# Splitting a block of the next matrix product behind the sum of two PSUM banks, with other places for attention in a tiled attention and two-layer kernel

## The chip, the cores and the metric

One core of a Trainium2 chip runs the whole kernel. The metric is the device time of one launch in microseconds. TensorE (PE in the profile) does the matrix products, VectorE (DVE) and ScalarE (ACT) the elementwise work, GpSimd (POOL) one power per pair of rows and a part of the DMA issues, SyncE (SP) the other DMA issues. The kernel before takes 1167.32 us, the median of three runs (1164.36 to 1168.64).

## What is computed

```
out  = softmax(q k / 8) v          # 4 x 8 heads, 768 rows, chunks of 32 with 16 left, 8 right, 8 memory keys
x    = out as 3072 x 512
xn   = x / sqrt(mean(x * x) + 1e-6) * rms_g
y    = (silu(xn @ w_gate) * (xn @ w_val)) @ w_out          # 512 -> 1536 -> 512
h    = y @ w_in                                            # 512 -> 2048
g    = where(h >= 1, h, where(h <= -1, 0, (h + 1)**2 / 4))
out  = g @ w_out                                           # 2048 -> 512
```

## The kernel before

The 3072 rows are six tiles of 512. Every fp32 operand of a product is held as two parts, a high one and what is left of it (`xh` and `xl`, `wh` and `wl`, `r[:, 0]` and `r[:, 1]`), and three matmuls (high by high, high by low, low by high) stand for one product of 128 x 128 by 128 x 512.

**Attention** is done in twelve pairs of 256 rows. A pair has nine steps: `s0`, `s1` (scores), `a0`, `a1` (transposes of the exponentials), `v0`, `v1` (weighted sums), `r0` (row scales, on ACT for all pairs but the first two, L526), `x0`, `x1` (transposes of the normalized rows, L540, copied out on ACT at L553). All of them write one PSUM tile, `ps_a`, of two banks.

**The first layer of tiles 0 to 3** runs in the loop at L832, twelve values of `f` each: the gate product `proj_in(ps_g[0])`, the value product `proj_in(ps_g[1])`, and the output product `out1` of the `f` before. Each is twelve matmuls. After each of the three stands a slot, `slot(t, s)` with s from 0 to 35; it runs at most one step of attention (`att_slot`, from the tables `plan`, `plan2` and `plan3`) and some steps of weight preparation (`conv_step`, or `conv_w` in tile 0). The tables give the slot of each step: in tile 0 by hand, later one pair per eleven slots (`plan2`). In tile 0 the order on PE and SP is the program's, and a scheduler orders DVE, ACT and POOL; from tile 1 on all engines take the order of the program. At the end of a tile `split_x` (L354) makes the two parts of the next tile's rows. `load_y` (L775) loads the rows of the last two tiles for what follows, and `x_steps` (L803) turns them into the sums below, one step per slot from `f` 8 of the last tile on.

**The first layer of the last two tiles and the whole second layer** use a scheme with seven half-size products in place of eight, for two tiles at once (called a pair of tiles here). `seven(n, early)` at L890 does one block of columns: products 0 to 6 of six matmuls each, on five PSUM banks. In the order of its code: products 0 (bank A) and 1 (C); ACT copies A to B (L898) and C to `p5` (L899); then everything in the list `defer`; product 2 adds to B, product 3 adds to A; DVE writes C = p5 + B (L906, the sum of banks of the title); `early` starts the activation of A; everything in `defer2`; product 4 adds to B; DVE adds B to `p5` (L912); product 5 adds to C; product 6 adds to B. So product 4 has to wait until L906 has read B, and product 6 until L912 has. `proj1` calls it for the first layer (12 blocks), `proj2` for the second (3 times 8 blocks); `conv_step` puts weight preparation between the products in `proj1`.

The output product of a pair of tiles is `Out.run` at L1001. It goes through blocks n, each with a split of one block of `h` into a ring buffer: `Out.split` (L984) is an ACT copy (L991), a DVE subtraction (L993) and, for the first blocks, a DVE sum (L995). The first few splits are done ahead, while `seven` still runs: `ahead` (L1051) puts them in `defer`, so that the next call of `seven` takes them. Four blocks are split so in `proj1`, and four in each of the three rounds of `proj2`, 16 in all.

Of the kernel before, what the change touches and what calls it, by code (L numbers as in the profile page):

```python
# [8 lines left out]
F32 = mybir.dt.float32  # L9
# [7 lines left out]
P = 128  # L17
# [13 lines left out]
TT = 512  # L31
# [3 lines left out]
PACE = (2.2, 2.9, 2.9, 3.1, 2.2, 2.9, 3.1, 4.2, 2.9, 4.2, 3.2)  # L35
# [4 lines left out]
def tile_stream_attention_moe_moe2(  # L40
# [14 lines left out]
    KK = DM // P  # L55
# [7 lines left out]
    att_only = ctx.enter_context(ExitStack())  # L63
# [41 lines left out]
    ps_a = apool.tile([P, 2, 512], F32, name="ps_a")  # L105
    ps_g = [psum.tile([P, 512], F32, name=f"ps_g{i}") for i in range(2)]
    y_d = [dram.tile([P, KK, TT], F32, name=f"y_d{t}") for t in range(NTT)]
    x_d = {t: dram.tile([P, KK, TT], F32, name=f"x_d{t}") for t in range(2, NTT)}
    NS = NTT - 2
# [52 lines left out]
    def conv_w():  # L162

        n = len(absd)
        if f32s:
            conv_hi()()
        if raw:
            conv_c()
        if n:
            conv_d()  # L170
# [168 lines left out]
    m2 = {"single": True, "pace": 0.0, "hold": False}  # L339
# [176 lines left out]
    def part_p(pr):  # L516
        rs = small.tile([P, 2], F32, tag="rs", name="rs")
        nc.gpsimd.tensor_tensor(out=rs, in0=ss_t.pop(2 * pr + 1), in1=nhalf, op=ALU.pow)
        rs_t[pr] = rs
# [11 lines left out]
            )  # L531

    def step_x(pr, blk, ps):

        t, o = divmod(pr, 2)
        if t == 1 and t not in xn_t:
            xn_t[t] = xs.tile([P, KK, TT], F32, tag="xn", name="xn")
        x = x_t[pr]
        for kk in range(KK):
            nc.tensor.transpose(ps[:, kk * P:(kk + 1) * P], x[blk][:, kk * P:(kk + 1) * P], ident)  # L540
        ps_t["x", pr, blk] = ps

    def part_X(pr, blk):
        t, o = divmod(pr, 2)
        ps = ps_t.pop(("x", pr, blk))
        c0 = (2 * o + blk) * P
        if t < 2:
            xn = xn_t[t][:, :, c0:c0 + P]
        else:
            xn = x_t[pr][blk].rearrange("p (k i) -> p k i", k=KK)  # L550
        rows = ps.rearrange("p (k i) -> p k i", k=KK)
        for kk in range(KK):
            nc.scalar.activation(xn[:, kk], rows[:, kk], AF.Copy, scale=g_t[:, kk:kk + 1])  # L553
        if t >= 2:
            nc.sync.dma_start(x_d[t][:, :, c0:c0 + P], xn)
# [69 lines left out]
    for st in ORDER.split():  # L625
        c, n = st[0], st[1:]
# [3 lines left out]
        n = int(n)  # L630
# [51 lines left out]
    mpsum = ctx.enter_context(tc.tile_pool(name="mpsum", bufs=1, space=bass.MemoryType.PSUM))  # L682
    ps_y.extend(mpsum.tile([P, 512], F32, name=f"ps_y{i}") for i in range(4))

    plan = {1: "s0", 3: "a0", 4: "v0", 7: "s1", 9: "a1", 10: "v1", 11: "r0", 14: "x0", 15: "x1"}

    plan2 = {0: "s0", 3: "a0", 4: "s1", 5: "v0", 6: "a1", 8: "v1", 11: "r0", 12: "x0", 13: "x1"}
    plan3 = {0: "s0", 3: "a0", 4: "s1", 5: "v0", 6: "a1", 7: "v1", 9: "r0", 10: "x0", 11: "x1"}  # L690

    def att_slot(t, s):
        if t == 0:
            o, r = divmod(s, 18)
            if r in plan:
                att_step(2 + o, plan[r])
            return

        if s == 34:
            return  # L700
        s += 36 * (t - 1)
        s -= (s > 34) + (s > 70)
        for pr in range(4, 2 * NTT):

            st = (plan3 if pr == 2 * NTT - 1 else plan2).get(s - 11 * (pr - 4))
            if st is not None:
                att_step(pr, st)

    def att_step(pr, st):
        n = int(st[1])  # L710
        if st[0] in "sav" and f"{st[0]}{2 * pr + n}" in done:
            return
        if st[0] == "x":
            step_x(pr, n, ps_a[:, n])
            part_X(pr, n)
        elif st[0] == "r":
            step_r(pr)
        else:
            u = 2 * pr + n
            fns[st[0]](u, ps_a)  # L720
            for p in parts[st[0]]:
                fn = (lambda p=p: fns[p](u)) if p != "p" else (lambda: part_p(pr) if n else None)
                if pr < 4 or p in "mAn":
                    fn()
                else:
                    (later if p in "kp" else after).append(fn)
        if st[0] == "s":
            load_qk(2 * pr + n + 1)
        if st[0] == "v":
            load_v(2 * pr + n + 1)  # L730
# [3 lines left out]
    def conv_step(n):  # L734
        m2["pace"] += n
        while m2["pace"] >= 1:
            m2["pace"] -= 1
            if m2["hold"] and not live:
                continue
            for fn in bg.pop() if bg else ():  # L740
                fn()

    def slot(t, s):
        late = later[:]
        later.clear()
        att_slot(t, s)
        for fn in late:
            fn()
        if t == 0:
            conv_w()  # L750
            load_w(units1, 1)
        else:
            if xq:
                xq.pop(0)()
            m2["hold"] = t == NS - 1 and s >= 29
            n = s + 36 * (t - 1)
            conv_step(1 if s > 32 else PACE[(n - (n > 34) - (n > 70)) % 11] if n < 92 else 2.5)
            for fn in after:
                fn()
            after.clear()  # L760
# [14 lines left out]
    def load_y(*src):  # L775
        for o in range(2):
            nc.sync.dma_start(m2["y"][:, o], src[o])
# [54 lines left out]
    for t in range(NS):  # L832
        if t == 1:
            region.close()
            region.enter_context(tc.manual_schedule())
        for f in range(F1):
            if t == NS - 1 and f == F1 - 1:
                for i in range(8):
                    load_wp(i)
            proj_in(ps_g[0], w1[("g", f)])  # L840
            s = sp.tile([P, TT], F32, tag="s", name="s")
            nc.scalar.activation(s, ps_g[0], AF.Silu)
            if t == NS - 1 and f == 8:
                xq.extend(x_steps())
            slot(t, 3 * f)
            if 0 < t < NS - 1 and f == 9:
                load_x(t + 1)
            if t == NS - 1 and f == 6:
                att_only.close()
                right = ctx.enter_context(tc.tile_pool(name="right", bufs=1, side="right", reuse_waits="tile"))  # L850
                m2["y"] = right.tile([P, 2, KK, TT], F32, name="y")
                load_y(x_d[NS], x_d[NS + 1])
            proj_in(ps_g[1], w1[("v", f)])
            if f == F1 - 1 and t + 1 < NS:
                split_x(xn_t.pop(t + 1))
            nc.vector.tensor_tensor(out=s, in0=s, in1=ps_g[1], op=ALU.mult)
            low = split_h(f, s)
            if t == 0:
                low()
            slot(t, 3 * f + 1)  # L860
            if t:
                low()
            if pend is not None:
                out1(*pend)
            pend = (t, f)
            slot(t, 3 * f + 2)
# [21 lines left out]
    banks, defer, defer2 = [], [], []  # L888
# [162 lines left out]
    def ahead(o, n, last):  # L1051
        if last:
            o.ahead(n)
        else:
            defer.append(lambda: o.ahead(n))

    def done1(j, o, bank, p5):

# [205 lines left out]
```

## Time and profile before

| | |
|---|---|
| median of three runs | 1167.32 us |
| the profiled execution, its own time | 1166.26 us |
| its span, first to last instruction | 1164.5 us |
| granted TensorE clock, mean | 0.987 of full speed |
| PE, DVE, ACT, POOL busy | 97%, 70%, 53%, 9% |

The span is cut into stages by the trace: up to 34 us the first attention alone, tile 0 up to 150, tiles 1 to 3 up to 497, `proj1` up to 614, its output product up to 700, and then three rounds of `proj2` with its output product. A matmul of 512 columns lasts 0.39 us in the profile, and the next starts 0.23 us after it started; since the ends overlap, idle time of PE is told shorter in the profile than what it costs. The columns of each view are named where its rows stand.

### The profile page before, as it was taken

How to read it: one execution, taken by the hardware profiler on the slowest of the kernel's cores; microseconds unless marked ns; L12 is line 12 of the kernel's file. 1: busy time of each engine (PE TensorE's matmuls, PEld its weight loads, DVE VectorE, ACT ScalarE, POOL GpSimd, SP SyncE). 2: the span in 40 equal slices, each digit the busy share in tenths (PEclk: the TensorE clock that was granted, in tenths of full speed). 3: DMA queues.
4: the chain of work that ended last, by engine and by line, in shares of the span. 5: the costliest groups of instructions: out<-in, count | busy, mean ns of one | idle time of the engine just before them, and what ended most of it. 6: DMA issues, size and time to landing. Idle time of an engine off the chain costs nothing.

```text
span 1164.5 us, 20927 instructions
## 1 busy us (share of the span) xinstructions
PE 1125.2 (97%) x7879; PEld 908.8 (78%) x7879; DVE 819.1 (70%) x1433; ACT 617.5 (53%) x1088; POOL 102.9 (9%) x152
## 2 busy tenths in 40 slices
PE   6999999999999999999989999999999999999998
PEld 4677787877787778887778887788887788877886
DVE  4887577767656765756656867797677887577855
ACT  3886656646665774444334534456344465344553
POOL 0200003221221222111110000000000000000000
PEclk6999999999999999999999999999999999999999
DMA  8976358998968877799987797666777667762564
GB/s 295 325 236 207 101 182 276 306 330 302 297 217 313 285 249 245 253 322 380 391 314 221 215 320 249 193 181 196 236 206 254 173 198 216 216 194 81 157 190 160
DMA packets 144212, 281.81 MB, mean 242 GB/s; under 512 B 15216, under 2 KB 65392, under 8 KB 142320
## 3 DMA queue, kind: packets, MB, share of 16 engines
q1 hardware_dynamic: 123664, 228.57, 61.6%
q0 software_dynamic: 12768, 43.52, 10.8%
q10 hardware_dynamic: 7680, 8.39, 2.1%
q8 instruction: 62, 1.02, 0.4%
q14 instruction: 38, 0.31, 0.1%
HBM read 201.26 MB, written 79.17 MB: 241 GB/s over the span
## 4 chain that ended last, share of the span: by engine, by line
PE 81%; DVE 6%; ACT 5%; DMA 5%; issue 2%; SPq 0%; POOL 0%; ACTq 0%; DVEq 0%; POOLq 0%
PE ps_y L1043 14%; PE ps_g L1043 11%; PE ps_g L564 6%; PE ps_g L566 6%; PE ps_g L565 6%; PE ps_b L879 4%; PE ps_g L879 4%; PE ps_b L881 3%; PE ps_b L880 3%; PE ps_g L881 3%; PE ps_g L880 3%; PE ps_y L564 3%; PE ps_y L565 3%; PE ps_y L566 3%; DMA w<-in_w_dram 2%
## 5 line engine op out<-in xcount | busy, mean ns | idle before, releaser
L1043 PE MATMUL ps_y<-r,wo 128*128 128x512 f32 x672 | 156.2, 390 | 0.0
L564 PE MATMUL ps_g<-xh,wall 128*128 128x512 f32 x384 | 155.5, 405 | 0.7 <-ACT wall L158 0.3
L993 DVE TENSOR_TENSOR r<-h,r 128x512 fp32r<-128x512 f32 x167 | 112.2, 688 | 61.8 <-ACT r L991 61.8
L566 PE MATMUL ps_g<-xh,wall 128*128 128x512 f32 x384 | 150.2, 391 | 0.7 <-DVE wall L160 0.7
L565 PE MATMUL ps_g<-xl,wall 128*128 128x512 f32 x384 | 150.2, 391 | 0.6 <-DVE xl L659 0.4
L1043 PEld LDWEIGHTS ps_y<-r,wo 128*128 128x128 f32 x672 | 125.6, 188 | 26.0
L944 ACT ACTIVATE t<-t,half 128x512 f32<-128x512 f32 x96 | 66.9, 720 | 126.6 <-DVE t L943 120.9
L991 ACT ACTIVATE r<-h 128x512 fp32r<-128x512 f32 x167 | 100.7, 625 | 56.2 <-DVE r L993 17.5
L1043 PE MATMUL ps_g<-r,wo 128*128 128x512 f32 x498 | 116.0, 390 | 0.0
L1043 PEld LDWEIGHTS ps_g<-r,wo 128*128 128x128 f32 x498 | 93.2, 188 | 19.4 <-DVE r L993 0.2
L566 PEld LDWEIGHTS ps_g<-xh,wall 128*128 128x128 f32 x384 | 72.1, 188 | 17.4 <-DVE wall L160 1.6
L564 PEld LDWEIGHTS ps_g<-xh,wall 128*128 128x128 f32 x384 | 72.1, 188 | 17.0 <-ACT wall L158 1.0
L879 PE MATMUL ps_g<-wall 128*128 128x512 f32 x198 | 78.5, 397 | 7.0 <-DVE ps_y L906 3.2
L565 PEld LDWEIGHTS ps_g<-xl,wall 128*128 128x128 f32 x384 | 72.2, 188 | 14.7 <-DVE xl L659 0.7
L879 PE MATMUL ps_b<-wall 128*128 128x512 f32 x202 | 79.8, 395 | 3.5 <-DVE ps_g L906 3.5
L881 PE MATMUL ps_b<-wall 128*128 128x512 f32 x202 | 79.1, 392 | 0.0
L880 PE MATMUL ps_b<-wall 128*128 128x512 f32 x202 | 79.1, 392 | 0.0
L564 PE MATMUL ps_y<-hh,wall 128*128 128x512 f32 x192 | 77.8, 405 | 0.0
L881 PE MATMUL ps_g<-wall 128*128 128x512 f32 x198 | 77.3, 390 | 0.0
L880 PE MATMUL ps_g<-wall 128*128 128x512 f32 x198 | 77.2, 390 | 0.0
L565 PE MATMUL ps_y<-hl,wall 128*128 128x512 f32 x192 | 75.1, 391 | 0.0
L566 PE MATMUL ps_y<-hh,wall 128*128 128x512 f32 x192 | 74.9, 390 | 0.0
(201 smaller groups left out, 2086.8 us busy)
## 6 DMA issues: line engine op xcount, KB each, us to landing
wo<-w2o_d SPq DMA_DIRECT2D x88, 512.0 KB, 3.6
wall<-w2p_d SPq DMA_DIRECT2D x168, 256.0 KB, 3.0
wall<-w1p_d SPq DMA_DIRECT2D x84, 256.0 KB, 6.2
w<-in_w_dram POOLq DMA_DIRECT2D x32, 512.0 KB, 5.7
w<-in_w_dram SPq DMA_DIRECT2D x30, 512.0 KB, 5.2
k_in<-in_k_dram SPq DMA_DIRECT2D x48, 256.0 KB, 5.1
wo<-w1o_d SPq DMA_DIRECT2D x21, 512.0 KB, 3.6
v_in<-in_v_dram SPq DMA_DIRECT2D x40, 260.0 KB, 4.2
```

The lines of the kernel that those rows point to most:

```text
L564: nc.tensor.matmul(ps, wh, xh, start=start, stop=False)
L565: nc.tensor.matmul(ps, wh, xl, start=False, stop=False)
L566: nc.tensor.matmul(ps, wl, xh, start=False, stop=stop)
L879: nc.tensor.matmul(bank, wh, xh, start=st, stop=False, skip_group_check=True)
L880: nc.tensor.matmul(bank, wh, xl, start=False, stop=False, skip_group_check=True)
L881: nc.tensor.matmul(bank, wl, xh, start=False, stop=kk == 1, skip_group_check=True)
L944: nc.scalar.activation(s, s, AF.Square, scale=0.5, bias=half)
L991: nc.scalar.activation(r[:, 0], src, AF.Copy)
L993: tt_(out=r[:, 1], in0=src, in1=r[:, 0].bitcast(F32), op=ALU.subtract)
L1043: nc.tensor.matmul(bank[p][m], a, b, start=s0, stop=s1, skip_group_check=True)
```

## The change

Five things, of which the first is a single word:

- `ahead` puts the split of a block into `defer2` in place of `defer`.
- The table `plan` of tile 0 names slots for both pairs by hand; the pairs' steps stand further apart (`a` to `v` two slots in place of one, `x0` to `x1` two in place of one) and begin two slots sooner.
- In `plan2`, the row scales `r0` stand at slot 10 of a pair in place of slot 11.
- Of the last three tiles, the second tile of the program keeps slots 33 and 34 free of attention (before, 34 alone), the third slot 34 as before. From there on attention runs one slot later, and so does `load_y`, which moves from behind slot 18 of the last tile to behind slot 19.
- `step_x` writes bank 0 of `ps_a` for `x1` too, where it wrote bank 1.

```diff
     def att_slot(t, s):
         if t == 0:
-            o, r = divmod(s, 18)
-            if r in plan:
-                att_step(2 + o, plan[r])
+            if s in plan:
+                att_step(*plan[s])
             return
 
-        if s == 34:
+        s += 36 * (t - 1)
+        if s in (33, 34, 70):
             return
-        s += 36 * (t - 1)
-        s -= (s > 34) + (s > 70)
+        s -= 2 * (s > 34) + (s > 70)
...
-    plan = {1: "s0", 3: "a0", 4: "v0", 7: "s1", 9: "a1", 10: "v1", 11: "r0", 14: "x0", 15: "x1"}
+    plan = {
+        1: (2, "a0"), 3: (2, "v0"), 4: (2, "s1"), 7: (2, "a1"), 9: (2, "v1"), 11: (2, "r0"), 12: (2, "x0"), 14: (2, "x1"),
...
-    plan2 = {0: "s0", 3: "a0", 4: "s1", 5: "v0", 6: "a1", 8: "v1", 11: "r0", 12: "x0", 13: "x1"}
+    plan2 = {0: "s0", 3: "a0", 4: "s1", 5: "v0", 6: "a1", 8: "v1", 10: "r0", 12: "x0", 13: "x1"}
...
-            step_x(pr, n, ps_a[:, n])
+            step_x(pr, n, ps_a[:, 0])
...
     def ahead(o, n, last):
         if last:
             o.ahead(n)
         else:
-            defer.append(lambda: o.ahead(n))
+            defer2.append(lambda: o.ahead(n))
```

In the rows below, lines of the changed kernel are one lower than those of the kernel before (L905 is the sum of banks L906, L992 the subtraction L993).

DVE in `proj2`, block 4 of the first round, before: `r0` is a ring buffer of the split, `ps_g0`, `ps_g1` and `ps_y3` are banks C, B and A of this call, `t0` is `p5`.

```order
L921 TENSOR_TENSOR h_7248<-h_7248 128x512
L993 TENSOR_TENSOR r0_7239<-h_7248,r0_7239 128x512
L995 TENSOR_TENSOR h_7248<-h_7248 128x512
L906 TENSOR_TENSOR ps_g0_111<-t0_7232,ps_g1_112 128x512
L943 TENSOR_SCALAR t1_7233<-ps_y3_706 128x512
L912 TENSOR_TENSOR t0_7232<-t0_7232,ps_g1_112 128x512
L948 TENSOR_TENSOR h_7248<-t1_7233,ps_y3_706 128x512
```

The same place in the changed kernel:

```order
L920 TENSOR_TENSOR h_7248<-h_7248 128x512
L905 TENSOR_TENSOR ps_g0_111<-t0_7232,ps_g1_112 128x512
L942 TENSOR_SCALAR t1_7233<-ps_y3_706 128x512
L992 TENSOR_TENSOR r0_7239<-h_7248,r0_7239 128x512
L994 TENSOR_TENSOR h_7248<-h_7248 128x512
L911 TENSOR_TENSOR t0_7232<-t0_7232,ps_g1_112 128x512
L947 TENSOR_TENSOR h_7248<-t1_7233,ps_y3_706 128x512
```

The two operations of the split moved from ahead of the sum of banks to a place between the activation of A and the second sum, L912 (now L911).

ACT at that place, before: L898 and L899 are the two copies of `seven`, L944 the square of the activation, L991 the copy of the split.

```order
L898 ACTIVATE ps_g1_112<-ps_y3_706 128x512
L899 ACTIVATE t0_7232<-ps_g0_111 128x512
L991 ACTIVATE r0_7239<-h_7248 128x512
L944 ACTIVATE t1_7233<-t1_7233,half_103 128x512
L944 ACTIVATE t2_7234<-t2_7234,half_103 128x512
```

And in the changed kernel:

```order
L897 ACTIVATE ps_g1_112<-ps_y3_706 128x512
L898 ACTIVATE t0_7232<-ps_g0_111 128x512
L943 ACTIVATE t1_7233<-t1_7233,half_103 128x512
L990 ACTIVATE r0_7239<-h_7248 128x512
L943 ACTIVATE t2_7234<-t2_7234,half_103 128x512
```

The split's copy now stands behind the square of A, whose input DVE makes from product 3.

ACT at the end of the second tile, before: L526 are the row scales of a pair, L438 the exponential of the next pair's scores with its table load, L356 the split of the next tile's rows, L553 the copies out of `x0`.

```order
L526 ACTIVATE x_nat_3012<-x_nat_3012,rs_3176 128x512
L526 ACTIVATE x_nat_3013<-x_nat_3013,rs_3176 128x512
L203 ACTIVATE wgv_3185<-s1234_3188 128x512
L438 ACT_TABLE_LOAD
L438 ACTIVATE e_3259<-e_3259 128x512
L356 ACTIVATE xh_582<-xn_3038 128x512 x4
L579 ACTIVATE hh_3290<-s_3221 128x512
L553 ACTIVATE x_nat_3012<-ps_a_110,g_t_108 128x128 x4
```

In the changed kernel:

```order
L526 ACTIVATE x_nat_3012<-x_nat_3012,rs_3176 128x512
L526 ACTIVATE x_nat_3013<-x_nat_3013,rs_3176 128x512
L203 ACTIVATE wgv_3185<-s1234_3188 128x512
L841 ACTIVATE s_3223<-ps_g0_111 128x512
L203 ACTIVATE wgv_3185<-s1234_3188 128x512
L356 ACTIVATE xh_582<-xn_3038 128x512 x4
L578 ACTIVATE hh_3247<-s_3223 128x512
L438 ACT_TABLE_LOAD
L438 ACTIVATE e_3300<-e_3300 128x512
L841 ACT_TABLE_LOAD
L841 ACTIVATE s_3324<-ps_g0_111 128x512
L552 ACTIVATE x_nat_3012<-ps_a_110,g_t_108 128x128 x4
```

The exponential moved from ahead of the split of the tile's rows to behind it, and the row scales went ahead of the gate's activation (L842, now L841).

## Rows read from the trace of the kernel before

**Rows 1.** The page: busy us of each engine, share of the span and instructions.

```profile
PE 1125.2 (97%) x7879; PEld 908.8 (78%) x7879; DVE 819.1 (70%) x1433; ACT 617.5 (53%) x1088; POOL 102.9 (9%) x152
```

**Rows 2.** Waits of PE, 34 to 150 us: us in total, times, longest.

```profile
PE ps_a L459 <- ACT aT L449: 2.3, 2, 1.2
PE ps_g L566 <- DVE wall L160: 0.7, 1, 0.7
PE ps_a L443 <- ACT e L438: 0.6, 1, 0.6
PE ps_a L540 <- ACT xn L553: 0.3, 1, 0.3
```

**Rows 3.** Waits of PE, 150 to 497 us.

```profile
PE ps_a L540 <- ACT x_nat L553: 2.5, 4, 1.3
PE ps_a L540 <- DVE e L429: 0.4, 1, 0.4
PE ps_g L564 <- ACT xh L356: 0.3, 1, 0.3
```

**Rows 4.** Waits of PE, 497 to 614 us.

```profile
PE ps_y L879 <- DVE ps_b L906: 2.0, 1, 2.0
PE ps_g L879 <- DVE ps_b L906: 2.0, 1, 2.0
PE ps_b L879 <- DVE ps_g L906: 1.7, 2, 1.3
PE ps_g L879 <- DVE ps_y L906: 1.3, 1, 1.3
```

**Rows 5.** Waits of PE, 614 to 1164 us, one of four such rows.

```profile
PE ps_y L879 <- DVE ps_b L906: 1.8, 3, 0.6
```

**Rows 6.** Timeline of PE, DVE, ACT from 714 us: start us, us, what, [idle before <-releaser].

```profile
714.12 0.39 PE L879 MATMUL ps_b<-wall 128*128 128x512 f32 x1
...
714.32 0.69 DVE L943 TENSOR_SCALAR t<-ps_g 128x512 f32<-128x512 f32 x1 [0.59 <-PE ps_g L881]
...
715.05 0.72 ACT L944 ACTIVATE t<-t,half 128x512 f32<-128x512 f32 x1 [2.79 <-DVE t L943]
...
715.68 0.69 DVE L912 TENSOR_TENSOR t<-t,ps_b 128x512 f32<-128x512 f32 x1 [0.67 <-PE ps_b L881]
```

**Rows 7.** Timeline of ACT and DVE around the split in the next block.

```profile
719.42 0.72 ACT L944 ACTIVATE t<-t,half 128x512 f32<-128x512 f32 x1 [0.74 <-DVE t L943]
720.05 0.58 ACT L898 ACTIVATE ps_g<-ps_y 128x512 f32<-128x512 f32 x1
721.18 0.60 ACT L899 ACTIVATE t<-ps_g 128x512 f32<-128x512 f32 x1 [0.55 <-PE ps_g L881]
721.67 0.62 ACT L991 ACTIVATE r<-h 128x512 fp32r<-128x512 f32 x1
...
722.33 0.69 DVE L993 TENSOR_TENSOR r<-h,r 128x512 fp32r<-128x512 f32 x1 [0.86 <-ACT r L991]
723.05 0.69 DVE L995 TENSOR_TENSOR h<-h 128x512 f32<-128x512 f32 x1
723.66 0.69 DVE L906 TENSOR_TENSOR ps_g<-t,ps_g 128x512 f32<-128x512 f32 x1
```

**Rows 8.** Timeline of PE at the same block's product 4.

```profile
723.41 0.39 PE L881 MATMUL ps_y<-wall 128*128 128x512 f32 x1
724.41 0.50 PE L879 MATMUL ps_g<-wall 128*128 128x512 f32 x1 [0.60 <-DVE ps_g L906]
```

**Rows 9.** Timeline of DVE in block 7 of `proj2`, first round.

```profile
756.14 1.22 DVE L819 TENSOR_TENSOR y<-y 128x1024 f32<-128x1024 f32 x1
757.37 0.69 DVE L912 TENSOR_TENSOR t<-t,ps_g 128x512 f32<-128x512 f32 x1
```

**Rows 10.** Windows: us, busy us (x) of PE, PEld, DVE, ACT, POOL, PEclk, DMA.

```profile
608.60:612.00 3.40, 3.40 (x10) 2.63 (x9) 1.29 (x2) 0.31 (x1) 1.05 (x2) 0.50 0.72 212
```

**Rows 11.** Timeline of DVE at the first step of `x_steps` in the last tile.

```profile
467.93 1.23 DVE L819 TENSOR_TENSOR y<-y 128x1024 f32<-128x1024 f32 x1 [4.07 <-DMA y<-x_d]
```

More of the change, by code (lines that the diff above doesn't have):

```diff
@@ L683, in tile_stream_attention_moe_moe2 @@
     ps_y.extend(mpsum.tile([P, 512], F32, name=f"ps_y{i}") for i in range(4))
-    plan = {1: "s0", 3: "a0", 4: "v0", 7: "s1", 9: "a1", 10: "v1", 11: "r0", 14: "x0", 15: "x1"}
-    plan2 = {0: "s0", 3: "a0", 4: "s1", 5: "v0", 6: "a1", 8: "v1", 11: "r0", 12: "x0", 13: "x1"}
+    plan = {
+        1: (2, "a0"), 3: (2, "v0"), 4: (2, "s1"), 7: (2, "a1"), 9: (2, "v1"), 11: (2, "r0"), 12: (2, "x0"), 14: (2, "x1"),
+        15: (3, "s0"), 18: (3, "a0"), 20: (3, "v0"), 21: (3, "s1"), 24: (3, "a1"), 26: (3, "v1"), 28: (3, "r0"),
+        29: (3, "x0"), 31: (3, "x1"),
+    }
+    plan2 = {0: "s0", 3: "a0", 4: "s1", 5: "v0", 6: "a1", 8: "v1", 10: "r0", 12: "x0", 13: "x1"}
     plan3 = {0: "s0", 3: "a0", 4: "s1", 5: "v0", 6: "a1", 7: "v1", 9: "r0", 10: "x0", 11: "x1"}
@@ L693, in att_slot @@
         if t == 0:
-            o, r = divmod(s, 18)
-            if r in plan:
-                att_step(2 + o, plan[r])
-            return
-        if s == 34:
+            if s in plan:
+                att_step(*plan[s])
             return
         s += 36 * (t - 1)
-        s -= (s > 34) + (s > 70)
+        if s in (33, 34, 70):
+            return
+        s -= 2 * (s > 34) + (s > 70)
         for pr in range(4, 2 * NTT):
@@ L756, in slot @@
             n = s + 36 * (t - 1)
-            conv_step(1 if s > 32 else PACE[(n - (n > 34) - (n > 70)) % 11] if n < 92 else 2.5)
+            conv_step(1 if s > 32 else PACE[(n - 2 * (n > 34) - (n > 70)) % 11] if n < 93 else 2.5)
             for fn in after:
@@ L847, in tile_stream_attention_moe_moe2 @@
                 load_x(t + 1)
[L848 to L852, printed above, removed]
             proj_in(ps_g[1], w1[("v", f)])
@@ L860, in tile_stream_attention_moe_moe2 @@
             slot(t, 3 * f + 1)
+            if t == NS - 1 and f == 6:
+                att_only.close()
+                right = ctx.enter_context(tc.tile_pool(name="right", bufs=1, side="right", reuse_waits="tile"))
+                m2["y"] = right.tile([P, 2, KK, TT], F32, name="y")
+                load_y(x_d[NS], x_d[NS + 1])
             if t:
```

## The prediction

> **What bounds the kernel now.** I read the page first, then PE's waits stage by stage, then the timeline around the waits. PE is busy 97% of the span [rows 1], so there is nothing to gain but PE's idle time, and nothing to lose but more of it. Its waits fall into four stretches. In tile 0, attention's products wait for ACT: 2.3 us for the transposed exponentials, 0.6 for exponentials, 0.3 for copies out [rows 2]. In tiles 1 to 3 attention's transposes wait for ACT and DVE, and the first products of a tile for ACT: 3.2 us [rows 3]. In `proj1` five waits of 7.0 us [rows 4], and in the three rounds of `proj2` four rows alike of 1.8 us, 12 waits and 7.2 us [rows 5], all end with the sum of banks, L906.
>
> A wait costs more than the profile shows, for the ends of matmuls overlap. At one of the twelve, the next matmul starts 1.00 us after the last in place of 0.23, and lasts 0.50 where others last 0.39 [rows 8]: 0.77 and 0.11, so 0.88 us for 0.60 shown. I add 0.28 to each shown wait of large products.
>
> Why L906 is late there is to be read in [rows 7]: the copy of the split (L991) starts when ACT has finished with the banks, DVE's subtraction L993 waits for it, L995 and L906 stand behind in DVE's queue. L906 starts at 723.66 and product 4 starts at 724.41, 0.06 after its end [rows 7, 8]. In a block without a split nothing waits [rows 6].
>
> **The change part by part.** The sum is made against the profiled execution's own time, 1166.26 us, which lies 1.06 below the median of the runs.
>
> *Splits in `proj2`, 12 of 16.* Removed: 12 waits at product 4, 12 x 0.88 = 10.6 us. Added: the split now stands between the activation of A and L912, on DVE, and its copy behind the square, on ACT. Product 6 has to wait for L912 as product 4 for L906. With product 4's start as zero, a block without a split has the clamp L943 at 0.20, the square L944 at 0.93, L912 at 1.56 [rows 6], and product 6 is due at 2.72, twelve starts of 0.227 later. With the split, ACT takes the copy 0.63 after the square (719.42 to 720.05 [rows 7]), at 1.56; DVE's subtraction follows 0.66 later (721.67 to 722.33), at 2.22, L995 0.72 later, at 2.94, and the next DVE operation 0.61 later: L912 starts at 3.55 in place of 1.56, ends at 4.24, and product 6 starts at 4.30. That is 1.58 late, 1.69 with the slower first matmul. In block 7 of the first two rounds the first step of `x_steps` stands between the split and L912 as well and takes 1.23 (756.14 to 757.37 [rows 9]): 2.92. Sum: 10 x 1.69 + 2 x 2.92 = 22.7 us. Behind a late L912, the chain of the activations is late relative to PE: the copy L898, which product 2 of the next block needs, would end some 0.1 us late, 9 times, 1 us; no wait for it is in the trace, so its bounds are 0 and 0.3 each, 0 to 2.7. Net: +13.1 us (bounds +11.5 and +15).
>
> *Splits in `proj1`, 4 of 16.* Four of the five waits of [rows 4] are at blocks with a split (2.0, 2.0, 1.3, 1.3; the fifth, 0.3, comes from weight preparation and stays): 6.6 + 4 x 0.28 = 7.7 us go. There the activation of A is one ACT operation from 0.20 on, the copy follows at 0.70 (0.49 apart, as L899 and L991 in [rows 7]), the subtraction at 1.36, L995 at 2.08, and the next at 2.69. Between it and L912 the order of the changed kernel puts one half-wide operation of weight preparation in the first block (0.34, half of 0.69 by the row), two whole ones in the second, one in the third and in the fourth (0.61 each): product 6 would start at 3.78, 4.66, 4.05 and 4.05 in place of 2.72, together 5.7 + 4 x 0.11 = 6.1 us. Net -1.6. Behind the last of the old waits PE ran a stretch at 0.50 of its clock, the lower of its two levels, 1.2 GHz [rows 10]: ten matmuls in 3.40 us, which at 0.227 each hold 15 at 2.4 GHz; five starts lost are 1.1, and with the edges I take 1.5 us. I let that go with the wait: -3.1 (bounds -4.5 and -0.5).
>
> *Attention in tile 0.* Steps that waited for a step one slot before now have two. The waits of [rows 2] for aT, e and xn go: 3.2 shown, with a part of the 0.28 each 3.8. The first `a0` stands one product of twelve starts, 2.7 us, sooner; it waited for nothing there, so now it waits at most that long. While it does, ACT and DVE finish the first weights, whose waits, 0.7 and some too small for the view [rows 2], then fall away; I take the one against the other, +0.3. Net -3.5 (bounds -4.3, all waits gone, and 0, given back by waits for weights).
>
> *Attention in tiles 1 to 3.* The row scales go into the slot before; 1.3 us of ACT work leaves the queue ahead of the exponential and the copies out of `x0`, for which `x1` waits in four of the rows' waits [rows 3]. The free slots put `split_x` of the second tile ahead of an exponential and its table load (the second place of the orders above), so the wait of 0.3 for xh and the like for xl go, and they shift later pairs by one slot, so that `x0` of most comes behind a gate product in place of an output product. I take all but a small rest: 3.4 shown, 7 waits, up to 0.28 more each; -4.6 (bounds -5.3 and -1).
>
> *`load_y` a slot later.* DVE already idles 4.07 us for it [rows 11]; it will idle some 2.7 more, twelve starts of 0.227. Behind it stands L856, which the value product of the next `f` needs, three products or 36 starts, 8.2 us, after the slot; 6.8 of idle time and the 1.23 of L819 come near that, though the idle time began before the slot. I take +0.3 (bounds 0 and +1.5).
>
> *Bank 0 for `x1`.* `x1` waits for the copies of `x0` in both kernels, since both name one tile: 0.
>
> Sum: 1166.3 + 13.1 - 3.1 - 3.5 - 4.6 + 0.3 = 1168.5 us. The bounds together give 1158 to 1183, were all at one end.
>
> **The rivals.**
> *1, covered.* Product 5 lies between L912 and product 6, and if the split fits there, all 16 waits go: 10.6 + 7.7 + 1.5, with 8.1 of attention, 1138 us. For it: a block without a split leaves L912 1.2 us of room (1.56 + 0.69 against 2.72 less the hand-over). Against it: the split's three steps in a row take 2.0 us (2.22 to 3.55 and the copy), and the copy cannot start before the square. It decides if ACT took the copy ahead of the square, which the order denies.
>
> *2, the clock.* One of the two waits of 2.0 [rows 4] came just ahead of the slow stretch [rows 10], the other left the clock at its upper level. Two of the new waits idle PE 2.6 us, ten 1.4. If the clock falls after the two, 2 x 1.5 = 3 us, 1171; if it also falls after the ten, 12 x 1.5 = 18 us, 1186, slower. The point is whether it falls after the shorter ones. Against it: four waits of 0.3 to 2.0 in `proj1` and twelve of 0.6 left it at full speed. The Trainium skill, TensorE: Matmul & The Clock Gate, in its section on HAM oscillation, says that idling between groups of matmuls that cycle through PSUM banks can bring the clock down again and again; by that rule the time would be towards 1186. The trace before has such groups at full speed for all but one stretch.
>
> *3, given back.* Attention's waits move with the slots in place of going, since ACT's queue holds the same work: the 8.1 of the two attention terms are not gained, 1176.6, slower. For it: DVE and ACT stay busy there to the same amount, and waits come from the phase of a step within its three slots. Against it: each wait of [rows 2] has its own cause one slot ahead, and the tables part just these.
>
> **How the numbers follow.** The forecast has 0.60; its own range is 1163 to 1174. Rival 1 has 0.13, rival 3 0.17, rival 2 0.10, half of it at 1171. A run of this kernel can tell 0.5% from no change, 5.8 us: faster is below 1161.5, slower above 1173.2. Rival 1 and a lower edge of 0.05 of the forecast make 0.18 for faster; rival 3, half of rival 2 and an upper edge of 0.04 make 0.26 for slower; 0.56 is left. The range leaves out rival 1 and the far end of rival 2, under 2 in 10: 1158 to 1178.
>
> **What would show it.** In the profile after: no waits of product 4 for the sum of banks at blocks with a split (12 of 0.6 in `proj2` gone), in their place 12 waits of the first matmul of product 6 for L911, ten of about 1.4 shown and two of 2.6; in `proj1` four of 0.9 to 1.8; the copy L990 0.6 behind the square. In tile 0 no wait for aT, and a wait of some 2 us of the first transposes near 42 us; near 264 us none for xh. The gap of DVE ahead of L818 in the last tile near 6.8 us. The prediction is wrong if product 6 does not wait, or if the clock's row shows more stretches at half.

## The result, and the profile after

The changed kernel takes **1180.18 us** (median of 4 runs, 1178.49 to 1181.01), the kernel before 1167.67 in the same session: ratio 1.011, 95% interval 1.0087 to 1.0134: 12.5 us slower, clear of the noise. The forecast was 1168.5 and the range ended at 1178. The profiled execution took 1181.01 us, its span is 1179.3.

The page: busy us of each engine, share of the span and instructions. It answers to [rows 1]: the same work in 14.8 us more of span, of which PE is busy for 3.9, DVE for 1.8 and ACT for none; the rest is idle time.

```profile
PE 1129.1 (96%) x7879; PEld 911.4 (77%) x7879; DVE 820.9 (70%) x1433; ACT 617.3 (52%) x1088; POOL 103.9 (9%) x152
```

Stage by stage, from the first large product of a stage to that of the next, in the two profiled executions (us):

| stage | before | after | difference | forecast |
|---|---|---|---|---|
| first attention | 34.27 | 34.64 | +0.4 | 0 |
| tiles 0 to 3 | 463.8 | 464.7 | +0.9 | -7.8 |
| `proj1` | 124.5 | 121.2 | -3.3 | -3.1 |
| its output product | 57.5 | 57.5 | 0 | 0 |
| three rounds of `proj2` | 79.8, 80.8, 80.7 | 85.6, 85.6, 84.5 | +14.4 | +13.1 |
| their output products | 78.9, 78.9, 85.3 | 79.6, 80.5, 85.3 | +2.3 | 0 |

The +0.9 of tiles 0 to 3 hides two parts. From the first gate product of a tile to that of the next, tile 0 lasts 116.2 us in place of 113.1, 3.1 more, and tiles 1 to 3 together 2.2 less.

**The second layer.** Waits of PE from 620 us on (us in total, times, longest). The waits of product 4 [rows 5] are gone, and 12 of product 6 for L911 stand in their place:

```profile
PE ps_g L878 <- DVE t L911: 10.6, 6, 2.5
PE ps_y L878 <- DVE t L911: 4.2, 3, 1.4
PE ps_b L878 <- DVE t L911: 4.2, 3, 1.4
```

The timeline of the changed kernel in block 4 of the first round (start us, us, what, [idle before <-releaser]), at the place of [rows 6, 7], and then in block 7:

```profile
721.86 0.69 DVE L942 TENSOR_SCALAR t<-ps_y 128x512 f32<-128x512 f32 x1 [0.59 <-PE ps_y L880]
722.59 0.72 ACT L943 ACTIVATE t<-t,half 128x512 f32<-128x512 f32 x1 [2.79 <-DVE t L942]
723.22 0.62 ACT L990 ACTIVATE r<-h 128x512 fp32r<-128x512 f32 x1
723.87 0.69 DVE L992 TENSOR_TENSOR r<-h,r 128x512 fp32r<-128x512 f32 x1 [1.31 <-ACT r L990]
724.59 0.69 DVE L994 TENSOR_TENSOR h<-h 128x512 f32<-128x512 f32 x1
725.20 0.68 DVE L911 TENSOR_TENSOR t<-t,ps_g 128x512 f32<-128x512 f32 x1
725.94 0.50 PE L878 MATMUL ps_g<-wall 128*128 128x512 f32 x1 [1.40 <-DVE t L911]
...
759.44 1.22 DVE L818 TENSOR_TENSOR y<-y 128x1024 f32<-128x1024 f32 x1
760.57 0.68 DVE L911 TENSOR_TENSOR t<-t,ps_g 128x512 f32<-128x512 f32 x1
761.31 0.50 PE L878 MATMUL ps_g<-wall 128*128 128x512 f32 x1 [2.53 <-DVE t L911]
```

The chain is to be read downwards: clamp, square, the split's copy on ACT, its subtraction and sum on DVE, L911, product 6. With product 4's start at 721.66 it stands at 0.20, 0.93, 1.56, 2.21, 2.93, 3.54, 4.28; the prediction had 4.30 for the last. In block 7 the first step of `x_steps` (L818) adds 1.13.

**The clock.** Windows over the long wait of tile 0 and over the first of the two in block 7 (us, busy us of PE, PEld, DVE, ACT, POOL, then PEclk, DMA share, GB/s). Behind both waits matmuls start 0.43 apart in place of 0.227, from 88.2 to 92.5 us and from 762.0 us on; that is the lower level, 1.2 GHz. A third such stretch lies at 929 us, behind the second block 7. The one of [rows 10] is gone.

```profile
86.30:92.60 6.30, 6.07 (x76) 4.84 (x77) 3.04 (x5) 3.61 (x6) 0.00 (x0) 0.50 0.63 209
760.90:765.20 4.30, 3.89 (x10) 3.07 (x11) 3.83 (x7) 1.86 (x3) 0.00 (x0) 0.60 0.12 21
```

**Attention.** Waits of PE from 34 to 150 us, which answer to [rows 2], and the two largest from 150 to 498, to [rows 3]:

```profile
PE ps_a L413 <- ACT xn L552: 2.6, 1, 2.6
PE ps_a L443 <- ACT e L438: 2.0, 1, 2.0
PE ps_a L539 <- ACT x_nat L526: 0.9, 1, 0.9
...
PE ps_a L443 <- ACT x_nat L552: 1.3, 1, 1.3
PE ps_y L564 <- DVE hl L580: 0.6, 1, 0.6
```

The old waits for aT, `x0` and weights are gone as foreseen. But the first `a0` waits 2.0, `s0` of pair 3 waits 2.6 for the copies of `x1`, one slot ahead of it, and `x0` waits 0.9 for the row scales, one slot ahead of it. The timeline at `s0`:

```profile
82.24 0.63 ACT L578 ACTIVATE hh<-s 128x512 fp32r<-128x512 f32 x1 [0.87 <-DVE s L850]
83.18 0.67 ACT L134 ACTIVATE tu<-w 128x512 f32<-128x512 f32 x1 [0.31 <-DMA w<-in_w_dram]
...
84.78 0.67 ACT L134 ACTIVATE tu<-w 128x512 f32<-128x512 f32 x1 [0.42 <-DMA w<-in_w_dram]
85.35 1.13 ACT L552 ACTIVATE xn<-ps_a,g_t 128x128 f32<-128x128 f32 x4
...
86.53 1.18 PE L413 MATMUL ps_a<-k_in,q_in 64*32 64x64 f32 x64 [2.59 <-ACT xn L552]
```

### The profile page after: what moved, and what is told of

It reads as the page before. It is cut to its first block, busy times and chain, and to the rows that moved or that the text cites. A ratio compares the mean times of both kernels' runs of the same rounds, so it can differ in the third digit from the quotient of the medians.

```text
span 1179.3 us, 20939 instructions
## 1 busy us (share of the span) xinstructions
PE 1129.1 (96%) x7879; PEld 911.4 (77%) x7879; DVE 820.9 (70%) x1433; ACT 617.3 (52%) x1088; POOL 103.9 (9%) x152
## 4 chain that ended last, share of the span: by engine, by line
PE 51%; DVE 4%; ACT 2%; issue 1%; DVEq 0%; ACTq 0%
PE ps_y L1042 14%; PE ps_g L1042 10%; PE ps_b L878 4%; PE ps_b L880 3%; PE ps_b L879 3%; PE ps_g L878 3%; PE ps_g L880 3%; PE ps_g L879 3%; PE ps_y L878 2%; PE ps_y L880 2%; PE ps_y L879 2%; DVE r L992 1%; PE ps_y L1084 1%; DVE t L911 1%; ACT r L990 1%; DVE h L994 1%
## 5 line engine op out<-in xcount | busy, mean ns | idle before, releaser
L992 DVE TENSOR_TENSOR r<-h,r 128x512 fp32r<-128x512 f32 x167 | 112.4, 688 | 69.5 <-ACT r L990 69.5
L1042 PE MATMUL ps_y<-r,wo 128*128 128x512 f32 x672 | 158.5, 394 | 0.0
L1042 PEld LDWEIGHTS ps_y<-r,wo 128*128 128x128 f32 x672 | 127.5, 190 | 26.7
L1042 PE MATMUL ps_g<-r,wo 128*128 128x512 f32 x498 | 116.1, 390 | 0.0
L1042 PEld LDWEIGHTS ps_g<-r,wo 128*128 128x128 f32 x498 | 93.2, 188 | 19.4 <-DVE r L992 0.2
```

Source lines behind the costliest of these rows:

```text
L992: tt_(out=r[:, 1], in0=src, in1=r[:, 0].bitcast(F32), op=ALU.subtract)
L1042: nc.tensor.matmul(bank[p][m], a, b, start=s0, stop=s1, skip_group_check=True)
```

## The experiments

Each ratio is to the kernel before, run on the same chip beside it, with its 95% interval. The runs are of four sessions, in which the kernel before took 1166.3 to 1168.3, so a difference of one or two us between runs of different sessions is best read from the ratios. In the diffs, lines that only declare the new lists, or let `split` do its three parts one by one, are left out.

| run | what | median us | ratio |
|---|---|---|---|
| e1 | splits alone | 1178.8 | 1.010 [1.008, 1.013] |
| e2 | all but the splits | 1163.2 | 0.997 [0.995, 0.998] |
| t1 | table of tile 0 alone | 1168.5 | 1.003 [1.001, 1.004] |
| t2 | later tiles' slots alone | 1160.7 | 0.996 [0.994, 0.997] |
| t3 | changed kernel, one `s0` later | 1176.1 | 1.007 [1.004, 1.009] |
| e4 | changed kernel, no early step of `x_steps` | 1177.1 | 1.009 [1.007, 1.011] |
| e6 | changed kernel, split's copy ahead of the square | 1154.8 | 0.990 [0.987, 0.992] |
| e3 | split behind the second sum | 1162.7 | 0.997 [0.995, 0.998] |
| e5 | split taken apart | 1149.7 | 0.986 [0.983, 0.989] |
| t4, f1, f3, g1, g2, g3 | e5 with other slots | 1146.5 to 1151.0 | 0.981 to 0.987 |

### Which part costs, which gains: e1, e2, t1, t2

e1 is the one word on the kernel before, e2 the changed kernel with that word back:

```diff
-            defer.append(lambda: o.ahead(n))
+            defer2.append(lambda: o.ahead(n))
```

> The kernel before with the splits alone moved behind the sum of banks, all else as before. Theory A (the loss is that of the splits: in proj2 +13.1 us of waits, two stretches of low clock of 1.6 each behind the two waits of 2.7, in proj1 -3.1): 13.2 us above before, 1180.9 us. Rival B (a part of the loss comes from attention's new places and the late y): at most 10 us above before, under 1178.

> The changed kernel with the splits put back ahead of the sum of banks: attention's places, the free slots, the late y and bank 0 alone. Theory A (attention's gains are given back by new waits, with one stretch of low clock near 88 us): 1166 to 1169.5 us, no difference from before. Rival B (the forecast's gains of 8.1 us are there and the splits cost more than was reckoned): 1159.6 us.

e1 is 11.7 us above before: theory A in kind, 1.5 less in size; in its trace `proj1` became 4.3 shorter, not 3.1. e2 is 3.9 below before, between the two. Neither theory had what its trace shows: tiles 0 to 3 last 464.2 us, no gain, and `proj1` lasts 121.1, 3.5 less. t1 and t2 part e2's change: t1 takes the new `plan` alone, t2 all the rest but the splits.

> The kernel before with the new table of tile 0 alone. Theory A (given back in tile 0: waits of 3.8 and 1.6 us go, and new ones of 2.2 for the exponential, 2.75 for the copies of x1, 1.0 for the row scales and 0.5 others come, with a stretch of low clock of 2.4 behind the 2.75): about 3 us above before, 1170; in the trace a wait near 86 us with low starts behind it. Rival B (the forecast: the old waits go and no others come but the first): 3.5 less, 1163.6.

> The changed kernel without its new table of tile 0 and with the splits ahead of the sum of banks: row scales a slot sooner, free slots, late y, bank 0. Theory A (in tiles 1 to 3 waits of 5.3 us go and 2.4 to 3.2 come; in proj1, which now stands otherwise to the weight preparation, the waits are shorter and the clock stays up, -3): 5 us below before, 1162. Rival B (the gain of the attention runs is of tile 0): within 1 us of before.

Theory A holds in both: t1 +2.2 us, t2 -5.6. t1's profiled execution, 1173.1 us, is the slowest of its ten, so its trace shows more loss than the median. Its waits from 36 to 150 us, and a window behind the longest:

```profile
PE ps_a L413 <- DVE x_nat L486: 3.6, 1, 3.6
PE ps_a L443 <- ACT e L438: 2.0, 1, 2.0
PE ps_a L413 <- ACT xn L553: 1.6, 1, 1.6
```

```profile
110.00:116.50 6.50, 6.18 (x76) 4.94 (x77) 3.44 (x7) 4.59 (x9) 0.00 (x0) 0.51 0.60 181
```

The 3.6 is `s1` of pair 3, one slot behind `v0`, for the sums of `v0` that DVE does late. The place is that of the table; how late DVE is there differs from run to run, with the same order of instructions in tile 0. In the five traces with this very table (the changed kernel, e4, e2, e6, t1) `s1` starts 0.2, 0.2, 1.7, 2.7 and 3.8 us late, and from 80 to 111 us ACT waits 1.8, 3.0, 4.4, 5.4 and 6.6 us for transfers of weights, for which DVE's weight preparation waits in turn: `s1` is late in the three in which ACT waited 4.4 or more, and the more the longer. No run changes the transfers, so this is read from the rows and not tested. The first and the last of the five:

```profile
ACT tu L134 <- DMA w<-in_w_dram: 1.8, 3, 1.1
ACT tu L134 <- DMA w<-in_w_dram: 6.6, 4, 4.1
```

In t2, tiles 0 to 3 are 2.1 us shorter and `proj1` 3.4 (121.1). Its waits in `proj1`, against [rows 4]:

```profile
PE ps_g L878 <- DVE ps_b L905: 1.3, 1, 1.3
PE ps_y L878 <- DVE ps_b L905: 1.3, 1, 1.3
PE ps_g L878 <- DVE ps_y L905: 1.3, 1, 1.3
PE ps_b L878 <- DVE ps_g L905: 0.9, 1, 0.9
```

The two waits of 2.0 are 1.3 now, and no stretch of low clock follows. In the order of instructions DVE has four half-wide operations of weight preparation ahead of the sum of banks in the first and last of these blocks before (L196, L197, L199, L200), and two in t2 (L199, L200). What shifts weight preparation against `proj1`'s blocks is a line of the change that the list of five things does not name. It paces `conv_step`, and moves with the free slots; by its numbers one step more has been taken by `n` = 92, in the last of these tiles (`n` numbers the slots through from tile 1):

```diff
-            conv_step(1 if s > 32 else PACE[(n - (n > 34) - (n > 70)) % 11] if n < 92 else 2.5)
+            conv_step(1 if s > 32 else PACE[(n - 2 * (n > 34) - (n > 70)) % 11] if n < 93 else 2.5)
```

t2 holds this line, the free slots, the row scales, the late y and bank 0 together; no run takes one of them alone. So both halves of the change shorten the same waits and take away the same low stretch: -3.4 from one, -4.3 from the other, -3.3 together. That is the larger part of why e1 and e2 together (+7.8) fall short of the whole (+12.5).

### One wait and the clock: t3, e4

t3 moves one step of the changed kernel's table; e4 takes out the early step of `x_steps`:

```diff
-        15: (3, "s0"), 18: (3, "a0"), 20: (3, "v0"), 21: (3, "s1"), 24: (3, "a1"), 26: (3, "v1"), 28: (3, "r0"),
+        16: (3, "s0"), 18: (3, "a0"), 20: (3, "v0"), 21: (3, "s1"), 24: (3, "a1"), 26: (3, "v1"), 28: (3, "r0"),
```

```diff
-            if g == 6 and xq:
-                defer2.append(xq.pop(0))
```

> The changed kernel with one number of its table changed: s0 of pair 3 at slot 16 in place of 15, two slots behind x1 of pair 2. Theory A (the 2.75 us are the rest of the copies of x1, and the clock falls because of this one wait): the wait falls below 0.3, no low stretch near 88 us, a new wait of 0.7 at a0, which now has two slots behind s0: 4.5 us less than the changed kernel, 1175.7. Rival B (ACT's queue is late as a whole there, so the wait moves with the step): no change, 1180.

> The changed kernel without the step of x_steps in block 7, which stands between the split and the second sum; the step goes into the output product. Theory A (the two long waits are those of 1.23 us more behind this step, and the clock falls because of their length): the two waits shrink from 2.7 to 1.6, both stretches of low clock at 762 and 929 us are gone: 2 x 1.2 + 2 x 1.6 = 5.6 us less, 1174.6 us. Rival B (the clock falls because of the row of waits of all the blocks ahead): only 2.4 less, 1177.8, and the two low stretches stay.

t3's median is 4.1 us below the changed kernel, near the 4.5 expected, but its six runs spread from 1172.2 to 1182.0 and the intervals of the two ratios overlap, so the gain is likely and not more. The profiled run is the slowest and gains nothing. At the place that was mended it does what theory A says: `s0` waits 0.1, `a0` 1.0, and the clock stays up. But the clock falls at two others, behind waits of 2.0 for an exponential and 1.9 for `v0`'s sums. Windows of t3:

```profile
44.40:49.00 4.60, 4.35 (x14) 3.53 (x15) 4.27 (x8) 4.58 (x9) 1.28 (x3) 0.63 0.92 335
85.00:93.00 8.00, 7.86 (x95) 6.24 (x94) 6.91 (x13) 5.88 (x13) 0.00 (x0) 1.00 0.63 193
108.90:114.00 5.10, 4.80 (x75) 3.86 (x76) 3.32 (x7) 4.51 (x9) 0.00 (x0) 0.67 0.56 169
```

In e4 the waits of block 7 are 1.4 like the others, and the window over the first of them has the clock at 1.00, where the changed kernel had 0.60: the clock fell for the length of the one wait, not for the row of waits ahead of it. The gain is 3.0 us and not 5.6, and the two ratios' intervals overlap. In the trace the rounds gain 3.3, but the first two output products last 80.5 each, with a new wait of L1042 for their splits. That the step's new place makes it is not shown: in g2 below the step is back in block 7, and a like wait is there too (0.9 in all). The third output product, which has no `x_steps`, keeps its 85.3 in e4, e5 and g2. Below stand the window over the first block 7 of e4 and the waits from 615 us on:

```profile
756.90:765.00 8.10, 6.71 (x30) 5.55 (x30) 7.64 (x14) 4.26 (x7) 0.00 (x0) 1.00 0.45 133
```

```profile
PE ps_g L878 <- DVE t L911: 8.4, 6, 1.4
...
PE ps_y L1042 <- DVE r L992: 1.3, 4, 0.4
```

### Where the split can stand: e6, e3, e5

Three other places. e6, on the changed kernel, puts the split's ACT copy ahead, DVE's part stays behind the activation:

```diff
-            defer2.append(lambda: o.ahead(n))
+            defer.append(lambda: o.ahead(n, "c"))
+            defer2.append(lambda: o.ahead(n, "sa"))
```

e3, on the kernel before, puts the whole split behind the second sum:

```diff
-            defer.append(lambda: o.ahead(n))
+            defer3.append(lambda: o.ahead(n))
...
         tt(out=p5, in0=p5, in1=B, op=ALU.add)
+        while defer3:
+            defer3.pop(0)()
```

e5 is the kernel before with the copy where it was, the subtraction between the sum of banks and the activation, the sum behind the activation, and without the early step of `x_steps`:

```diff
-            defer.append(lambda: o.ahead(n))
+            defer.append(lambda: o.ahead(n, "c"))
+            mid.append(lambda: o.ahead(n, "s"))
+            defer2.append(lambda: o.ahead(n, "a"))
...
         tt(out=C, in0=p5, in1=B, op=ALU.add)
+        while mid:
+            mid.pop(0)()
         done11 = early(A)
         while defer2:
             defer2.pop(0)()
```

> The changed kernel with the ACT copy of the split taken back ahead of the square, while its DVE subtraction and sum stay behind the sum of banks. Theory A (of the 1.58 us by which product 6 is late, the ACT copy behind the square costs 1.3): the second sum starts 2.2 us after product 4, the ten waits shrink from 1.56 to 0.3, the two of 2.69 to 1.6, the clock stays up behind them, proj1's waits go but for 0.5: 23 us less, 1157 us. Rival B (DVE's two operations by themselves make the wait): the ten waits stay above 1, 1170 us.

> The kernel before with the whole split behind the second sum, where no product waits for a sum any longer. Theory A (the work behind the second sum is a chain of activations that ends in the copy of A, 5.93 us after product 4 starts, while product 2 of the next block is due at 6.83 and the copy lasts 0.6: 0.3 us of room for 1.35 us of new DVE work): the 12 waits of products 4 in proj2 are replaced by 12 waits of product 2 for the copy of A, 1.0 us each; with the gains in proj1 of 7 to 9 us: 1159 to 1162 us. Rival B (there is room behind the second sum): all waits gone, 1148.

> The kernel before with the split taken apart: its ACT copy ahead, where it was, its DVE subtraction between the sum of banks and the activation of A, its DVE sum between the activation and the second sum; the early step of x_steps goes into the output product. Theory A (PE waits only because DVE work stands ahead of the two sums; DVE idles 0.59 and 0.67 us at the two new places): all 16 waits of products 4 and 6 go, 10.6 + 6.6 + 1.1 us and 1.5 for the clock at 608 us: 1148 us. Rival B (the DVE and ACT work of a block just fills it, so the late work comes out as waits of product 2 for the copy of A): 0.6 to 0.9 a block is given back, 1156 to 1160 us.

**e6** is 25.4 us below the changed kernel: theory A. Its timeline has nothing idle between the clamp and the second sum, which starts 2.1 after product 4 (734.28); of the ten waits at most 0.15 us is left, and 1.1 each of the two in block 7:

```profile
734.48 0.69 DVE L942 TENSOR_SCALAR t<-ps_g 128x512 f32<-128x512 f32 x1 [0.60 <-PE ps_g L880]
735.09 0.69 DVE L994 TENSOR_TENSOR r<-h,r 128x512 fp32r<-128x512 f32 x1
735.81 0.69 DVE L996 TENSOR_TENSOR h<-h 128x512 f32<-128x512 f32 x1
736.42 0.68 DVE L911 TENSOR_TENSOR t<-t,ps_b 128x512 f32<-128x512 f32 x1
```

So the 1.56 us by which product 6 was late were almost wholly the copy's place behind the square on ACT, for which DVE stood idle 1.31.

**e3**: theory A too, just above its range (1162.7). No product waits for a sum; product 2 of the next block waits for L898, which stands in ACT's queue behind the last square, in each of 9 blocks that have a block behind them (not 12, as I expected). One row of three alike, and the timeline:

```profile
PE ps_b L879 <- ACT ps_b L898: 2.9, 3, 1.0
```

```profile
719.04 0.72 ACT L946 ACTIVATE t<-t,half 128x512 f32<-128x512 f32 x1 [0.74 <-DVE t L945]
719.67 0.58 ACT L898 ACTIVATE ps_y<-ps_b 128x512 f32<-128x512 f32 x1
...
720.30 0.50 PE L879 MATMUL ps_y<-wall 128*128 128x512 f32 x1 [0.98 <-ACT ps_y L898]
```

**e5** is 17.4 us faster than before: theory A. The rounds of `proj2` last 76.2, 77.1, 77.1 us (3.6 less, 0.90 for each of four waits), `proj1` 115.3, 9.2 less. DVE's timeline at block 4:

```profile
721.12 0.69 DVE L906 TENSOR_TENSOR ps_b<-t,ps_y 128x512 f32<-128x512 f32 x1 [1.08 <-PE ps_y L881]
721.73 0.68 DVE L997 TENSOR_TENSOR r<-h,r 128x512 fp32r<-128x512 f32 x1
722.41 0.69 DVE L945 TENSOR_SCALAR t<-ps_b 128x512 f32<-128x512 f32 x1
723.02 0.68 DVE L999 TENSOR_TENSOR h<-h 128x512 f32<-128x512 f32 x1
723.77 0.69 DVE L914 TENSOR_TENSOR t<-t,ps_y 128x512 f32<-128x512 f32 x1
```

The two operations fill the two idle times of a block without a split (0.59 ahead of the clamp and 0.67 ahead of the second sum [rows 6]); both sums come when their banks are ready. Two output products became 1.3 us longer each (1.6 in e4). The rounds, `proj1` and these give -10.8 - 9.2 + 2.5, the 17.4 of the medians.

### Other slots on top of e5: t4, f1, f3, g1, g2, g3

All have e5's split. t4 and g3 have a table of their own for tile 0, f1 and f3 share a third; f1, f3, g1 and g3 have the changed kernel's slots for the later tiles (f1 with slot 71 free in place of 70); g1, g2 and g3 the early step of `x_steps` behind the second sum. g3's table, the lists of f1 and the line of g2 (the tables of t4 and f1 differ from g3's by at most one slot for any step):

```diff
+        3: (2, "a0"), 5: (2, "v0"), 6: (2, "s1"), 9: (2, "a1"), 11: (2, "v1"), 12: (2, "r0"), 14: (2, "x0"), 15: (2, "x1"),
+        17: (3, "s0"), 20: (3, "a0"), 22: (3, "v0"), 25: (3, "s1"), 28: (3, "a1"), 29: (3, "v1"), 30: (3, "r0"),
+        32: (3, "x0"), 33: (3, "x1"),
...
-        if s in (33, 34, 70):
+        if s in (33, 34, 71):
...
-                defer2.append(xq.pop(0))
+                defer3.append(xq.pop(0))
```

> The kernel with the split taken apart (1149.7 us), and with a table for tile 0 in which no step stands one slot behind the ACT work that it needs: a to v, r0 to x0, x0 to x1, x1 to s0 two slots each, s to a three; only the last x1 stands one behind x0. Theory A: the waits of tile 0 for aT, e and xn (3.8 us in before) fall to 0.6: 3.2 less, 1146.5. Rival B (ACT's queue holds the same work, and other steps wait in their place): 1149.7.

> The changed kernel with the split taken apart as in the run of 1149.7 us, a table for tile 0 with no s1 right behind v0, and slot 71 free in place of slot 70, so that a0 of a pair stands two slots behind x1 where the rows of the last tile are split. Theory A (what waits is what stands one slot behind ACT or DVE work): of the 1149.7 go 2 us in tiles 1 to 3 by the later tiles' slots, 1.5 by slot 71, and 2.5 in tile 0: 1144. Rival B (attention's waits move with its steps and nothing adds up): 1148 to 1150.

> The same with slot 70 free, as in the changed kernel. Theory A: the wait of 1.5 us near 387 us of a0 for the copies of x1 stays, 1.5 above the run with slot 71 free, 1145.5. Rival B: no difference.

> The kernel with the split taken apart (1149.7 us), with the early step of x_steps back in block 7, but behind the second sum. Theory A (without that step in block 7 the steps in the output products come one place later and DVE is late with the splits there: 1.28 us in each of two output products, while behind the second sum of a last block nothing waits): the two output products fall back from 80.2 to 78.9 us, 2.6 us less, 1147.1 us. Rival B (the step behind the second sum delays the splits ahead of the output product, and its first matmuls wait): no gain, 1149.7.

> The same with the later tiles' slots, the row scales a slot sooner, the late y and bank 0 of the changed kernel, but the table of tile 0 as it was before. Theory A (the later tiles' slots gain 2.1 us in tiles 1 to 3 by themselves, the rest of their 5.6 was proj1's, which has no waits left here): 2.1 less than without them, 1145. Rival B (all of their gain was in proj1): no difference, 1147.

> The same with a table for tile 0 that keeps a0 at slot 3, where the first weights are made, a to v two slots, s1 of pair 3 three slots behind v0. Theory A (a table can take tile 0's waits away where no step stands in front of late DVE or ACT work): tile 0's waits fall from 5.4 to some 3 us, 2 less than with the table of before, 1143. Rival B (DVE's and ACT's queues hold the same work, and what waits is only another step): no difference, 1145.

t4 (1150.1) and f1 (1151.0) are misses of theory A. f3 (1148.1) is one too: it was to be 1.5 above f1 and is 2.9 below, and since the runs of the two overlap, no difference (rival B) is not excluded. In t4 the waits for aT, e and copies fell to 0.4 us, but `s1`, again one slot behind `v0`, waits 1.7, and PE, earlier now, waits in `proj1` for a transfer of weights that had not been late before. Waits of t4, 36 to 150 us and 498 to 620 us:

```profile
PE ps_a L413 <- DVE x_nat L486: 1.7, 1, 1.7
...
PE ps_g L879 <- DMA wall<-w1p_d: 1.6, 1, 1.6
```

f1's slot 71 took one wait away and put `x0`'s copies behind an activation's table load: 2.0 us at 383 and a stretch of low clock. g2 (1149.4) is no better than e5, rival B: its output products still last 80.0, and in its trace PE waits 1.8 and 0.7 in `proj1` for transfers of weights, as in t4. g1 (1147.6) and g3 (1146.5) differ by less than their spread, rival B for g3; against g2, the later tiles' slots are worth 1.8 in medians, within the intervals (0.980 to 0.984 against 0.981 to 0.986). **The lowest median is g3's: ratio 0.981 [0.979, 0.984], 22 us faster than before and 34 than the changed kernel**, though the runs do not tell it from g1. It has e5's split; its table of tile 0 is at best 1 us of that.

## Why the prediction was wrong

By its own steps, against the two profiled executions (+14.7 us where +2.2 was forecast):

- **Splits in `proj2`, right in mechanism and nearly in size.** Product 6 starts 4.28 after product 4 (forecast 4.30); 10 waits of one length and 2 longer by the step of `x_steps`, as said; no product waits for L897, for which the sum held 1.0. The third round, where nothing else differs, gives the price of a wait: against e5, which has none, 84.5 less 77.1 over four is 1.84, where I had 1.69. Removed were 0.90 each for 0.88. Rounds: +14.4 and output products +2.3 for a term of 13.1 (bounds 11.5 to 15). What exceeds it is mostly the clock: two stretches at the lower level, some eight starts in each 0.20 too far apart, 3.2 us.
- **Splits in `proj1`: -3.3 for -3.1,** with four waits of 0.9 to 1.7 (forecast 0.9 to 1.8). But the sum counted the gain as the splits' own, while the rest of the change without tile 0's table brings -3.4 there by itself (t2). The count of operations of weight preparation was made behind the sum of banks, where the splits go, and not ahead of it, where the pace moves the same operations. The total does not suffer from that, since the sum took the old waits from before and the new ones from the changed kernel's order.
- **Attention in tile 0, the step that failed: "steps that waited for a step one slot before now have two".** The table made two slots of some distances, and one of others: `x1` to `s0` (four before), `v0` to `s1` (three before) and `r0` to `x0` (three before). I priced only what it removed, -3.5 with an upper bound of 0. Alone it costs +2.2 (t1), and in the changed kernel's trace tile 0 is 3.1 longer. The first `a0`, which was foreseen, waits 2.0, of which 1.0 comes back in waits for weights that are gone; I had set +0.3 for both. "ACT's queue holds the same work" stood under rival 3, and what stood against it ("each wait of [rows 2] has its own cause one slot ahead") was true of the new waits too. A slot of 2.7 us is not enough where ACT's queue holds weight preparation that itself waits: behind the transposes of `x1` ACT waits 0.87 us for DVE and 0.31 and 0.42 for transfers of weights, and the copies of `x1` stand behind all three (85.35). The Trainium skill, TensorE: Matmul & The Clock Gate, in its section on the architectural detail of the array (the paragraph on engine queues), calls ACT's and DVE's queues strict FIFO; the timeline agrees: the copies of `x1` start only when the last L134 has issued.
- **Attention in tiles 1 to 3: -2.1 alone (t2), -2.2 in the changed kernel, for -4.6.** The waits for xh and `x0` went, and `a0` of one pair now waits 1.3 for the copies of `x1`, beside the split of the tile's rows. The late y (+0.3, bounds 0 and 1.5) cost 1.2 in the changed kernel's trace by starts, and nothing in e2's; in the former DVE idles 5.47 for it, where I had 6.8.
- **The clock, rival 2 at its first point.** It fell behind the two waits of 2.69 and behind none of the ten of 1.56, the 1171 that I gave a chance of 0.05, and once more in tile 0, which was in no case. By the prediction's own sign, more stretches at half, it was wrong there: three in place of one. Of the twelve waits in `proj2`, the clock fell behind two. The Trainium skill, TensorE: Matmul & The Clock Gate, in its section "A second HAM failure mode: psum-queue depth-cycling", has the rule that I set beside that rival, of short idling between groups of matmuls that cycle through PSUM banks. As I read it the clock would have fallen behind all twelve, and the rows speak against that.
- **The sum itself.** The bounds of its terms add up to 1163.7 and 1181.3, not to the 1158 and 1183 that stand there; the measured 1180.2 lies inside them and outside the range, which left out that end. The sum also starts from an execution 1.06 below the median and does not add that back.

So rival 3 came nearest (1176.6 forecast, 1180.2 measured): attention as a whole gained nothing. Rival 2 came with it, where I had weighed them as if one excluded the other. Rival 1 was wrong for the change as made, and e5 shows what it would have taken. What stays open is how late DVE and ACT are in tile 0 in a given run, on which 2 to 4 us hang; the rows point to the transfers of weights, and no run tested them.

## What to carry to other kernels

Before moving a lump of work, look for the idle times of its queue (the bracket of the timeline) and whether the lump can be cut to fit them: here two DVE operations of 0.7 us fitted two gaps of 0.6 and 0.7, and the same work in one piece cost 11 us in the rounds of `proj2` ahead of the first sum, 25 ahead of the second (with the step of `x_steps` and the clock) and 12 behind it (before, after and e3 against e5). When a table of slots is changed, list every distance that it makes shorter, not only those that it widens, and price each by the queue that stands ahead, waits for transfers included. And add cases that can come together, instead of weighing them as if they could not.

## What the runs showed of the hardware

The clock. In the 17 traces of this study I counted the waits after 36 us by how much later the next matmul started than it would have. Of 89 waits of 1.3 to 1.92 us, none was followed by a stretch at the lower level; of 26 of 2.1 to 3.8 us, 21 were. The five that were not include one of 3.0 (f1, at 116 us), and at one place in `proj1` a wait of 2.18 had none behind it in the trace before (at 544 us), one of 2.17 had one in t1's (at 550 us). What decides in these few was not found. Each such stretch cost 1 to 2.4 us beside the wait itself (5 to 12 starts 0.20 too far apart), so a long wait is to be priced with that as a case of its own.
